# Attention scores on TensorE: one 64-row product per head in place of a block-diagonal product per pair of heads

## The chip, the core and the metric

The kernel runs on one core of a Trainium2 chip. Its engines work side by side, each with its own queue: PE (TensorE, the matrix unit; PEld is its loading of the stationary operand), DVE (VectorE), ACT (ScalarE), POOL (GpSimd) and SP (SyncE, which here only issues DMAs). The metric is the device time of one execution in microseconds (us); smaller is better.

## The reference

Attention with pooled keys and values is followed by a gated channel mix. There are 8 batches, 8 heads, 576 tokens and 64 elements per head. Keys and values are averaged over groups of 8 tokens, so that each head has 72 of each.

```python
k_p = k.reshape(B, H, Sp, pool, D).mean(axis=3)          # Sp = 72
v_p = v.reshape(B, H, Sp, pool, D).mean(axis=3)
scores = scale * np.matmul(q, k_p.transpose(0, 1, 3, 2)) # 576 x 72 per head, sum over 64
scores = scores - np.max(scores, axis=-1, keepdims=True)
attn = np.exp(scores)
attn = attn / (np.sum(attn, axis=-1, keepdims=True) + 1e-09)
x = np.matmul(attn, v_p)                                  # heads side by side: 512 wide
# channel mix, x_prev is x shifted by one token
xk = mu_k * x + (1.0 - mu_k) * x_prev
xr = mu_r * x + (1.0 - mu_r) * x_prev
k = np.maximum(xk @ w_k, 0.0)                             # 512 -> 1024
v = k * k @ w_v                                           # 1024 -> 512
out = 1.0 / (1.0 + np.exp(-(xr @ w_r))) * v
```

## The kernel before

The 8 x 576 = 4608 tokens are laid end to end and cut into 12 chunks of 384, and each chunk into three tiles of 128. 576 is four and a half tiles, so 4 of the 36 tiles hold the seam between two batches: 64 tokens of each. The other 32 are called whole tiles here.

A tile goes through `softmax(i)`: PE multiplies queries and pooled keys into two PSUM banks (`sc`), DVE takes the maximum of each head (L715) and subtracts it (L733), ACT takes the exponential (L738), DVE sums (L740, L743, L746), and DVE or POOL normalises. From the third chunk on the result is transposed on DVE in blocks of 32 (L780, L784), written to DRAM and fetched back turned; in the first two chunks PE transposes it (L826, and L881 for the last 8 keys of each head). `attended` multiplies with the pooled values on PE (L940), mixes with the shifted tokens on ACT, POOL and DVE (L946, L953, L966), and `x_parts` splits the result into a high and a low part (ACT L982, POOL L984). `hidden`, `gate` and `mixed` are the three weight products (L1011, L1063, L1094). In the first chunk they are true fp32 products (two passes of PE per product); later each is three fp32r products of one pass each, on the high and low parts.

The score product before: the pooled keys of a pair of heads stand in `kbd`, 128 rows by 144 columns, as two diagonal blocks (head 0 in rows 0 to 63 and columns 0 to 71, head 1 in rows 64 to 127 and columns 72 to 143; the rest is zeros, cleared once by a memset on L430). The queries of the pair, 128 rows by the tile's tokens, are the stationary operand. One fp32 product per pair gives both heads: four per whole tile, each two passes. On a seam tile there are four per half, with 64 columns of the array for each half; the program gives those the array shape 128 rows by 64 columns, and the halves alternate.

What sets the order: every engine runs its own queue in order. A planner (`Order`) makes the order while the program is built. Pieces of work are generators which tell what they need and what the next instruction costs; the planner takes the one that could start first by its costs, and among those the one with the earliest due time (the table `DUE`, and lead times such as `TILE_LEAD`). Loads are issued by SP in the order of `LOADS`, and each takes a free buffer first: `qs` has 3, so a fourth tile of queries cannot be issued before a score product has freed one, and all loads behind it in SP's queue stand still meanwhile. `SUM_BY` says which engine pools the keys and values of a batch (t: PE, v: DVE, g: POOL, L580), `NORM_BY` who normalises a tile (DVE or POOL), `BY_HEAD` the tiles whose exponentials ACT takes head by head (L724), and `LOW_BY` and `LAST_BITS_BY` who converts the weights.

The planner's price for a piece of PE work is built from these lines:

```python
def pe(n, whole=False, times=1):
    return "pe", times * (2 * max(0.109, n / 1200 + 0.002) if whole else max(0.109, n / 2383 + 0.0125)), False
```

For the scores of a part of a tile that is `pe(144, True, 4)`.

Of the kernel before, what the change touches and what calls it, by code (L numbers as in the profile page):

```python
# [8 lines left out]
F32 = mybir.dt.float32  # L9
# [4 lines left out]
ALU = mybir.AluOpType  # L14
# [27 lines left out]
    "k0 k1 q0 wr3 q2 q1 r0 c0 q3 wk0 wv6 k2 wk1 q5 v1 wk4 wv1 k3 wr2 v0 wr0 wk3 q4 wk5 v3 wk6 "  # L42
    "wk2 r1 wv3 wv4 wv2 wv5 wv7 wv0 v2 wk7 wr1 "
)

SUM_BY = {"k0": "t", "k1": "v", "v0": "t", "v1": "t", "r0": "t", "k2": "t", "k3": "t", "v2": "v", "v3": "g", "r1": "v", "k5": "v", "k4": "v", "v5": "v", "r2": "v", "v4": "g"}

NORM_BY = {0: "g", 1: "v", 2: "g", 3: "g", 7: "g", 5: "g", 4: "v", 8: "g", 6: "g"}
WARMING = 4
FILLS = ((("scored", 1), 7),)  # L50

LAST_BITS_BY = {"k": "aaavvvvv", "r": "vava", "v": "vaavaava"}
LOW_BY = {"k": "vvvggvgg", "r": "vvgv", "v": "vgvgvggg"}
BY_HEAD = (0, 2, 8)

BESIDE = (1,)
SQUARED_ON_ACT = 8
REST_BY = (1, 1, 1, 3)
# [29 lines left out]
    "constants": -31.16, "complements": 163.29, "fill 7": 127.28, "values 2 1": 57.34,  # L88
# [32 lines left out]
    "split_turned 8": 67.34, "split_turned 9": 136.19, "free_turned": -43.12, "fetch_turned 2": 63.7,  # L121
    "fill 2": -65.13, "split_turned 10": 147.03, "split_turned 11": 146.15, "softmax 14": 201.08,
    "keys 4 0": 355.88, "softmax 15": 188.81, "keys 4 1": 179.46, "softmax 16": 182.51,
}
SPARE = 3.109
SECOND = 24.0
FIRST = 22.0
PER_TOKEN = 0.1736
TILE_LEAD = 31.7186
ATT_LEAD = 34.7421  # L130


class Thread:
    __slots__ = ("due", "steps", "spare", "name", "at", "pe_at", "step", "last")

# [135 lines left out]
def act(n, func=None):  # L271
    return "act", 0.095 + n / 1200, False, func
# [11 lines left out]
def attention_then_channel_mix(  # L284
# [35 lines left out]

    full, low, high = {}, {}, {}

    kbd = [const.tile([P, NPAIR, 2 * KEYS], F32, name=f"kbd{i}") for i in range(2)]
    vbd_h = [const.tile([P, NPAIR, P], F32R, name=f"vbd_h{i}") for i in range(2)]
    vbd_l = [const.tile([P, NPAIR, P], F32R, name=f"vbd_l{i}") for i in range(2)]
    vbd_r = [const.tile([REM, 2, 4, D], F32R, name=f"vbd_r{i}") for i in range(2)]
# [887 lines left out]
```

## Time and profile before

| what | us |
|---|---|
| median of 3 runs (lowest, highest) | 623.45 (622.16, 623.87) |
| the profiled execution, its own time | 625.45 |
| span of the profile, first to last instruction | 623.6 |
| PE busy | 607.1 (97%) |
| DVE, ACT, POOL busy | 403.0, 363.7, 203.4 |

The profile gives one execution. Its own time lies 1.85 us above its span, and 2.0 us above the median. A busy time counts an instruction from its start to its modelled end; matmuls overlap, so the cost of one in a stream is read from the distance of the starts, not from its duration. A row of the timeline merges neighbours of one kind: start, length, engine, line, shape, count, and in brackets the idle time before it and what ended that. The shape 128*64 means 128 rows by 64 columns of the array.

### The profile page before, as it was taken

The numbers are of one execution on the slowest core, as the hardware profiler recorded it, in microseconds if no ns is written. First come the engines' busy times: TensorE is split into PE (matmuls) and PEld (weight loads), VectorE is DVE, ScalarE is ACT, GpSimd is POOL, SyncE is SP. The second block draws the span as 40 slices with busy tenths as digits, with TensorE's granted clock in tenths as the row PEclk, the third lists the DMA queues.
The fourth block names the chain that finished last, engine by engine and source line by source line (L and its number), as shares of the span: only waits on it lengthen the run. The fifth ranks groups of instructions, "written<-read, shape, count | busy, mean of one in ns | idle before, by whom it ended". The sixth has DMA issues, their size and how long they took to land.

```text
span 623.6 us, 8940 instructions
## 1 busy us (share of the span) xinstructions
PE 607.1 (97%) x3100; PEld 524.1 (84%) x3100; DVE 403.0 (65%) x826; ACT 363.7 (58%) x761; POOL 203.4 (33%) x292
## 2 busy tenths in 40 slices
PE   7789999999999999999999999999999999999997
PEld 6755457988988988988988988988988988988986
DVE  4789977975995844884884853794774753623511
ACT  4879975854575744774754753774654643633420
POOL 1130276326415215515614204713713313303100
PEclk9999999999899999999999999999999999999999
DMA  8997221562377132057147124049114013000001
GB/s 263 383 354 239 67 80 62 188 152 70 89 222 186 37 87 77 18 175 193 35 175 176 35 77 105 18 140 227 35 55 112 18 41 88 18 0 35 17 1 51
DMA packets 59453, 68.61 MB, mean 110 GB/s; under 512 B 11664, under 2 KB 43664, under 8 KB 59408
## 3 DMA queue, kind: packets, MB, share of 16 engines
q1 hardware_dynamic: 59264, 67.91, 36.6%
q8 instruction: 24, 0.39, 0.3%
q14 instruction: 21, 0.17, 0.1%
q10 hardware_dynamic: 144, 0.13, 0.1%
HBM read 49.75 MB, written 18.28 MB: 109 GB/s over the span
## 4 chain that ended last, share of the span: by engine, by line
PE 87%; DMA 5%; DVE 3%; POOL 2%; ACT 1%; issue 1%; SPq 0%; DVEq 0%; ACTq 0%; POOLq 0%
PE mm L1094 31%; PE mm L1011 29%; PE mm L1063 15%; PE bank L940 5%; PE sc L700 5%; DMA early_xrl<-in_vm 2%; DMA got_wk<-in_w_k 2%; DMA early_sl<-in_kT 1%; POOL xkl L984 1%; PE bank L448 1%; ACT t L946 1%; PE mm L591 1%; DVE xm L966 1%; POOL xrl L984 0%; ACT xkh L982 0%
## 5 line engine op out<-in xcount | busy, mean ns | idle before, releaser
L1011 PE MATMUL mm<-xkh,w_k 128*128 128x384 f32 x704 | 181.8, 339 | 1.5 <-ACT xkh L982 1.5
L1094 PE MATMUL mm<-w_v,sh 128*128 128x512 f32 x528 | 169.4, 391 | 0.0
L1011 PEld LDWEIGHTS mm<-xkh,w_k 128*128 128x128 f32 x704 | 127.1, 189 | 2.9 <-ACT xkh L982 1.7
L1011 PE MATMUL mm<-xkl,w_k 128*128 128x384 f32 x352 | 118.9, 338 | 1.7 <-POOL xkl L984 1.7
L1094 PEld LDWEIGHTS mm<-w_v,sh 128*128 128x128 f32 x528 | 99.2, 188 | 19.6
L1094 PE MATMUL mm<-w_v,sl 128*128 128x512 f32 x264 | 102.9, 390 | 0.0
L946 ACT ACTIVATE t<-bank,om_sb 128x384 f32<-128x384 f32 x96 | 49.8, 580 | 80.0 <-PE bank L940 78.7
L751 POOL TENSOR_TENSOR e<-e,sm 128x576 f32<-128x576 f32 x30 | 35.6, 1188 | 177.5 <-DVE sm L746 177.5
L1063 PE MATMUL mm<-w_r,xrh 128*128 128x512 f32 x264 | 84.2, 393 | 0.0
L1107 DVE TENSOR_TENSOR rs<-mm,rs 128x512 f32<-128x512 f32 (+1 forms) x37 | 24.9, 675 | 90.6 <-PE mm L1094 90.6
L966 DVE SCALAR_TENSOR_TENSOR xm<-bank,mu_sb,t 128x384 f32<-128x384 f32 x88 | 51.0, 611 | 36.9 <-POOL t L957 17.1
L1037 ACT CAST sh<-rk 128x384 fp32r<-128x384 f32 x88 | 44.8, 514 | 49.7 <-DVE rk L1031 49.4
L1011 PEld LDWEIGHTS mm<-xkl,w_k 128*128 128x128 f32 x352 | 66.6, 189 | 3.2 <-POOL xkl L984 3.2
L984 POOL TENSOR_TENSOR xkl<-xm,xkh 128x384 fp32r<-128x384 f32 x44 | 45.2, 1027 | 70.3 <-ACT xkh L982 70.1
L1039 DVE TENSOR_TENSOR sl<-rk,sh 128x384 fp32r<-128x384 f32 x88 | 51.8, 597 | 12.2 <-ACT sh L1037 10.5
L1063 PEld LDWEIGHTS mm<-w_r,xrh 128*128 128x128 f32 x264 | 49.6, 188 | 10.1
L1094 PEld LDWEIGHTS mm<-w_v,sl 128*128 128x128 f32 x264 | 49.6, 188 | 9.2
L1031 DVE SCALAR_TENSOR_TENSOR rk<-mm,rk 128x384 f32<-128x384 f32 x88 | 47.3, 548 | 11.1 <-ACT rk L1024 10.7
L1063 PE MATMUL mm<-w_r,xrl 128*128 128x512 f32 x132 | 51.4, 389 | 0.0
L1024 ACT ACTIVATE rk<-mm 128x384 f32<-128x384 f32 x88 | 42.2, 487 | 10.8 <-PE mm L1011 7.4
L984 POOL TENSOR_TENSOR xrl<-xm,xrh 128x384 fp32r<-128x384 f32 x44 | 45.6, 1036 | 3.3 <-ACT xrh L982 3.3
L580 POOL TENSOR_TENSOR stage<-stage 128x512 f32<-128x512 f32 (+5 forms) x51 | 45.0, 897 | 1.2
(126 smaller groups left out, 904.2 us busy)
## 6 DMA issues: line engine op xcount, KB each, us to landing
out<-rs SPq DMA_DIRECT2D x35, 256.0 KB, 2.0
passing<-pm SPq DMA_DIRECT2D x30, 288.0 KB, 2.2
qs<-in_qT SPq DMA_DIRECT2D x32, 256.0 KB, 3.6
stage<-in_kT SPq DMA_DIRECT2D x14, 576.0 KB, 4.7
turned_sb<-passing SPq DMA_DIRECT2D x40, 192.0 KB, 4.3
stage<-in_vm SPq DMA_DIRECT2D x14, 512.0 KB, 6.5
got_wk<-in_w_k SPq DMA_DIRECT2D x8, 512.0 KB, 9.0
got_wv<-in_w_v SPq DMA_DIRECT2D x8, 512.0 KB, 11.2
```

The lines of the kernel that those rows point to most:

```text
L580: nc_eng.tensor_tensor(out=st[:, :, :w], in0=st[:, :, :w], in1=st[:, :, w:2 * w], op=ALU.add)
L751: eng.tensor_tensor(out=e, in0=e, in1=sm.broadcast_to([P, 2, 4, KEYS]), op=ALU.mult)
L946: nc.scalar.activation(out=t[:, m, 1:n + 1], in_=xp, func=AF.Copy, scale=om_sb[:, m, g:g + 1])
L966: nc.vector.scalar_tensor_tensor(out=xm[:, :n], in0=xp, scalar=mu_sb[:, m, g:g + 1], in1=t[:, m, :n], op0=ALU.mult, op1=ALU.add,)
L984: nc.gpsimd.tensor_tensor(out=lo, in0=xm[:, :n], in1=hi, op=ALU.subtract)
L1011: nc.tensor.matmul(out=hp, lhsT=w[:, o], rhs=x[:, ct, o_t], start=(ct == 0 and k == 0), stop=(ct == NCT - 1 and k == len(terms) - 1),)
L1024: nc.scalar.activation(out=rk[:, :n], in_=hp, func=AF.Relu)
L1031: nc.vector.scalar_tensor_tensor(out=rk[:, :n], in0=hp, scalar=0.0, in1=rk[:, :n], op0=ALU.max, op1=ALU.mult)
L1037: nc.scalar.copy(out=sh, in_=rk[:, :n])
L1039: nc.vector.tensor_tensor(out=operand("sl", c)[:, jt, o_t], in0=rk[:, :n], in1=sh, op=ALU.subtract)
L1063: nc.tensor.matmul(out=bank, lhsT=x[:, ct, o], rhs=w, start=(ct == 0 and k == 0), stop=(ct == NCT - 1 and k == len(terms) - 1),)
L1094: nc.tensor.matmul(out=bank, lhsT=s[:, o], rhs=w, start=(jt == 0 and k == 0), stop=(jt == NJT - 1 and k == len(terms) - 1),)
```

## The change

The pooled keys become dense: `ks` holds, for each pair, head 0 in rows 0 to 63 and head 1 in rows 64 to 127, both in the same 72 columns. The score of each head is a product of its own over 64 rows: 8 products of 72 columns per part of a tile instead of 4 of 144. The two heads of a pair use the upper and the lower half of the array's rows and write to different banks (`halves[h2]`); the program gives these products the array shape 64 by 128 on whole tiles and 64 by 64 on seam tiles. The order on a seam tile is now part by part, and head by head inside a part. The layout of scores, exponentials and normalised tiles follows: even heads, then odd heads. One copy writes the keys of two pairs (before: two copies of 64 rows), and the memsets of `kbd` go. The planner is told 0.75 us per part (`SCORE`), and its tables differ.

```diff
 LOADS = (
-    "k0 k1 q0 wr3 q2 q1 r0 c0 q3 wk0 wv6 k2 wk1 q5 v1 wk4 wv1 k3 wr2 v0 wr0 wk3 q4 wk5 v3 wk6 "
-    "wk2 r1 wv3 wv4 wv2 wv5 wv7 wv0 v2 wk7 wr1 "
+    "k0 k1 q0 wr3 q1 q3 r0 c0 wk0 wv6 q2 v1 wk1 k2 wk4 k3 q5 wv1 v0 wr2 wk3 wk2 wr0 v3 q4 wk5 "
+    "wk6 v2 wv4 r1 wk7 wv5 wv2 wr1 wv7 wv0 wv3 "
 )
-SUM_BY = {..., "v2": "v", "v3": "g", ..., "r2": "v", "v4": "g"}
+SUM_BY = {..., "v2": "g", "v3": "g", ..., "r2": "v", "v4": "v"}
-NORM_BY = {0: "g", 1: "v", 2: "g", 3: "g", 7: "g", 5: "g", 4: "v", 8: "g", 6: "g"}
+NORM_BY = {0: "v", 1: "v", 2: "v", 3: "v", 7: "g", 5: "g", 4: "v", 8: "v", 6: "g"}
-FILLS = ((("scored", 1), 7),)
+FILLS = ((("scored", 1), 8),)
-LAST_BITS_BY = {"k": "aaavvvvv", "r": "vava", "v": "vaavaava"}
-LOW_BY = {"k": "vvvggvgg", "r": "vvgv", "v": "vgvgvggg"}
-BY_HEAD = (0, 2, 8)
+LAST_BITS_BY = {"k": "avavvavv", "r": "aava", "v": "vaavavvv"}
+LOW_BY = {"k": "vvvvvvvg", "r": "gvgg", "v": "vgvvgvgv"}
+BY_HEAD = (0, 2, 6, 8)
-SQUARED_ON_ACT = 8
+SQUARED_ON_ACT = 5
 DUE = {
-    "keys 0 0": -9.94, "values 0 0": 24.5, "keys 0 1": -129.19, "values 0 1": -72.82,
+    "keys 0 0": 81.0, "values 0 0": -2.56, "keys 0 1": -144.43, "values 0 1": -63.22,
...
-SPARE = 3.109
+SPARE = 2.8473
+SCORE = 0.75
-PER_TOKEN = 0.1736
-TILE_LEAD = 31.7186
-ATT_LEAD = 34.7421
+PER_TOKEN = 0.1794
+TILE_LEAD = 54.3891
+ATT_LEAD = 35.0556
...
-    kbd = [const.tile([P, NPAIR, 2 * KEYS], F32, name=f"kbd{i}") for i in range(2)]
+    ks = [const.tile([P, NPAIR, KEYS], F32, name=f"ks{i}") for i in range(2)]
...
-        for b in range(2):
-            yield "pool" if b else "dve", 0.6, False
-            (nc.gpsimd if b else nc.vector).memset(kbd[b], 0.0)
-            order.make(("kbd clear", b))
...
-        yield "act", 0.53, False
-        for h2 in range(2):
-            r = slice(h2 * D, (h2 + 1) * D)
-            nc.scalar.copy(out=kbd[b % 2][r, gs, h2 * KEYS:(h2 + 1) * KEYS], in_=o[r])
+        yield act(2 * KEYS)
+        nc.scalar.copy(out=ks[b % 2][:, gs], in_=o)
...
-        yield pe(2 * KEYS, True, NPAIR * len(parts))
-        for g in range(NPAIR):
-            k = (g % 2) * 2 * KEYS
-            for b, _, n, o in parts:
-                nc.tensor.matmul(
-                    out=halves[g // 2][o:o + n, 0, k:k + 2 * KEYS],
-                    lhsT=qs[:, g, o:o + n], rhs=kbd[b % 2][:, g, :], start=True, stop=True,
-                )
+        yield "pe", SCORE * len(parts), False
+        for b, _, n, o in parts:
+            for g in range(NPAIR):
+                for h2 in range(2):
+                    r = slice(h2 * D, (h2 + 1) * D)
+                    nc.tensor.matmul(
+                        out=halves[h2][o:o + n, 0, g * KEYS:(g + 1) * KEYS],
+                        lhsT=qs[r, g, o:o + n], rhs=ks[b % 2][r, g, :], start=True, stop=True,
+                    )
...
-        pairs = e.rearrange("p a (h two) k -> p (a h) two k", two=2)
         for h2 in range(2):
             nc.vector.transpose(
...
-                in_=pairs[:, :, h2, :KM].rearrange("p g (f j) -> p f g j", j=BLOCK),
+                in_=e[:, h2, :, :KM].rearrange("p g (f j) -> p f g j", j=BLOCK),
             )
```

The changed tables move instructions. Chunks are counted from 0. From chunk 4 on, the blocks of PE's queue stand as before, with 8 products in place of 4 per part of a tile; in chunks 2 and 3 two blocks of scores stand at another place between the weight products. Two other places differ where engines wait. The first is SP's queue at the start, right behind the small load of `mu_sb` (`qs` are queries, `got_wk` and `got_wv` weights, `in_kT` keys, `in_vm` values; the number tells the buffer). Before:

```order
L491 DMA mu_sb<-in_mu 128x8
L499 DMA qs_105<-in_qT 128x4x128
L509 DMA got_wk_174<-in_w_k 128x1024
L509 DMA got_wv_186<-in_w_v 128x1024
L523 DMA early_sl<-in_kT 128x1152
L509 DMA got_wk_191<-in_w_k 128x1024
```

With the change:

```order
L489 DMA mu_sb<-in_mu 128x8
L507 DMA got_wk_153<-in_w_k 128x1024
L507 DMA got_wv_156<-in_w_v 128x1024
L497 DMA qs_105<-in_qT 128x4x128
L521 DMA early_sl<-in_vm 128x1024
L507 DMA got_wk_186<-in_w_k 128x1024
```

The queries that reuse the first tile's buffer `qs_105` now stand behind two weights, where they stood ahead of them.

The second is POOL's queue while the inputs of chunk 2's weight products are made (`xkl` and `xrl` are low parts, `stage` the values of batch 2 on their way to being pooled, `t` the shifted tokens). Before:

```order
L984 TENSOR_TENSOR xrl_1208<-xm_82,xrh_1207 128x384
L580 TENSOR_TENSOR stage_108<-stage_108 128x2x256
L580 TENSOR_TENSOR stage_108<-stage_108 128x2x128
L580 TENSOR_TENSOR stage_108<-stage_108 128x2x64
L580 TENSOR_TENSOR stage_110<-stage_110 96x2x256
L953 COPY t_80<-carry 128x2
L580 TENSOR_TENSOR stage_110<-stage_110 96x2x128
L984 TENSOR_TENSOR xkl_1199<-xm_83,xkh_1198 128x384
```

With the change:

```order
L981 TENSOR_TENSOR xrl_1253<-xm_83,xrh_1252 128x384
L578 TENSOR_TENSOR stage_110<-stage_110 128x2x256
L578 TENSOR_TENSOR stage_110<-stage_110 128x2x128
L578 TENSOR_TENSOR stage_110<-stage_110 128x2x64
L578 TENSOR_TENSOR stage_108<-stage_108 96x2x256
L578 TENSOR_TENSOR stage_108<-stage_108 96x2x128
L578 TENSOR_TENSOR stage_108<-stage_108 96x2x64
L578 TENSOR_TENSOR stage_109<-stage_109 128x2x256
L950 COPY t_81<-carry 128x2
L981 TENSOR_TENSOR xkl_1244<-xm_82,xkh_1243 128x384
```

Seven sums stand between the last `xrl` of the third pair and the copy for the fourth, where four stood.

More of the change, by code (lines that the diff above doesn't have):

```diff
@@ L41 @@
 LOADS = (
-    "k0 k1 q0 wr3 q2 q1 r0 c0 q3 wk0 wv6 k2 wk1 q5 v1 wk4 wv1 k3 wr2 v0 wr0 wk3 q4 wk5 v3 wk6 "
-    "wk2 r1 wv3 wv4 wv2 wv5 wv7 wv0 v2 wk7 wr1 "
-)
-SUM_BY = {"k0": "t", "k1": "v", "v0": "t", "v1": "t", "r0": "t", "k2": "t", "k3": "t", "v2": "v", "v3": "g", "r1": "v", "k5": "v", "k4": "v", "v5": "v", "r2": "v", "v4": "g"}
-NORM_BY = {0: "g", 1: "v", 2: "g", 3: "g", 7: "g", 5: "g", 4: "v", 8: "g", 6: "g"}
+    "k0 k1 q0 wr3 q1 q3 r0 c0 wk0 wv6 q2 v1 wk1 k2 wk4 k3 q5 wv1 v0 wr2 wk3 wk2 wr0 v3 q4 wk5 "
+    "wk6 v2 wv4 r1 wk7 wv5 wv2 wr1 wv7 wv0 wv3 "
+)
+SUM_BY = {"k0": "t", "k1": "v", "v0": "t", "v1": "t", "r0": "t", "k2": "t", "k3": "t", "v2": "g", "v3": "g", "r1": "v", "k5": "v", "k4": "v", "v5": "v", "r2": "v", "v4": "v"}
+NORM_BY = {0: "v", 1: "v", 2: "v", 3: "v", 7: "g", 5: "g", 4: "v", 8: "v", 6: "g"}
 WARMING = 4
-FILLS = ((("scored", 1), 7),)
-LAST_BITS_BY = {"k": "aaavvvvv", "r": "vava", "v": "vaavaava"}
-LOW_BY = {"k": "vvvggvgg", "r": "vvgv", "v": "vgvgvggg"}
-BY_HEAD = (0, 2, 8)
+FILLS = ((("scored", 1), 8),)
+LAST_BITS_BY = {"k": "avavvavv", "r": "aava", "v": "vaavavvv"}
+LOW_BY = {"k": "vvvvvvvg", "r": "gvgg", "v": "vgvvgvgv"}
+BY_HEAD = (0, 2, 6, 8)
 BESIDE = (1,)
-SQUARED_ON_ACT = 8
-REST_BY = (1, 1, 1, 3)
+SQUARED_ON_ACT = 5
+REST_BY = (1, 1, 3)
 TURNED = 2
@@ L62 @@
 DUE = {
[25 rows of a table removed]
-    "constants": -31.16, "complements": 163.29, "fill 7": 127.28, "values 2 1": 57.34,
[32 rows of a table removed]
-    "split_turned 8": 67.34, "split_turned 9": 136.19, "free_turned": -43.12, "fetch_turned 2": 63.7,
-    "fill 2": -65.13, "split_turned 10": 147.03, "split_turned 11": 146.15, "softmax 14": 201.08,
-    "keys 4 0": 355.88, "softmax 15": 188.81, "keys 4 1": 179.46, "softmax 16": 182.51,
-}
-SPARE = 3.109
[58 rows of a table added]
+    "split_turned 7": 99.44, "split_turned 8": 73.38, "split_turned 9": 148.16, "free_turned": -68.37,
+    "fetch_turned 2": 53.56, "fill 2": -42.7, "split_turned 10": 156.94, "split_turned 11": 160.34,
+    "softmax 14": 181.95, "keys 4 0": 382.77, "softmax 15": 207.62, "keys 4 1": 196.24,
+    "softmax 16": 179.15,
+}
+SPARE = 2.8473
+SCORE = 0.75
 SECOND = 24.0
 FIRST = 22.0
-PER_TOKEN = 0.1736
-TILE_LEAD = 31.7186
-ATT_LEAD = 34.7421
+PER_TOKEN = 0.1794
+TILE_LEAD = 54.3891
+ATT_LEAD = 35.0556
 class Thread:
@@ L609, in keys @@
     def keys(b, p):
-        yield need(("k", 2 * b + p), *([("scored", last_tile[b - 2])] if b > 1 else [("kbd clear", b)]))
+        yield need(("k", 2 * b + p), *([("scored", last_tile[b - 2])] if b > 1 else []))
         kind, raw, o = yield from sums(held.pop(("k", 2 * b + p)), KEYS, SUM_BY.get(f"k{2 * b + p}", "v"))
         gs = slice(2 * p, 2 * p + 2)
-        yield "act", 0.53, False
-        for h2 in range(2):
-            r = slice(h2 * D, (h2 + 1) * D)
-            nc.scalar.copy(out=kbd[b % 2][r, gs, h2 * KEYS:(h2 + 1) * KEYS], in_=o[r])
+        yield act(2 * KEYS)
+        nc.scalar.copy(out=ks[b % 2][:, gs], in_=o)
         done_with(kind, raw)
@@ L756, in softmax @@
         got = yield take("pm")
-        pm = got[:, :8 * KM].rearrange("p (a h k) -> p a h k", a=2, h=4)
+        pm = got[:, :8 * KM].rearrange("p (g two k) -> p g two k", g=NPAIR, two=2)
         yield dve(8 * KR) if v else ("pool", 0.24, True)
         eng.tensor_tensor(
-            out=px, in0=e[:, :, :, KM:], in1=sm.broadcast_to([P, 2, 4, KR]), op=ALU.mult
+            out=px.rearrange("p a (g two) k -> p two (a g) k", two=2), in0=e[:, :, :, KM:], in1=sm.broadcast_to([P, 2, 4, KR]), op=ALU.mult
         )
@@ L765, in softmax @@
         eng.tensor_tensor(
-            out=pm, in0=e[:, :, :, :KM], in1=sm.broadcast_to([P, 2, 4, KM]), op=ALU.mult
+            out=pm.rearrange("p g two k -> p two g k"), in0=e[:, :, :, :KM], in1=sm.broadcast_to([P, 2, 4, KM]), op=ALU.mult
         )
@@ L781, in turned @@
                 out=u[:, h2 * 8 * BLOCK:(h2 + 1) * 8 * BLOCK].rearrange("p (f g j) -> p f g j", f=2, j=BLOCK),
-                in_=pairs[:, :, h2, :KM].rearrange("p g (f j) -> p f g j", j=BLOCK),
+                in_=e[:, h2, :, :KM].rearrange("p g (f j) -> p f g j", j=BLOCK),
             )
         nc.vector.transpose(
-            out=u[:, 16 * BLOCK:].rearrange("p (r h k) -> p r h k", r=2, k=KR), in_=e[:, :, :, KM:]
+            out=u[:, 16 * BLOCK:].rearrange("p (g two k) -> p g two k", two=2, k=KR),
+            in_=e[:, :, :, KM:].rearrange("p two g k -> p g two k"),
         )
@@ L827, in transposed @@
                 out=tp[:, g, :],
-                in_=pm[:, g // 2, (g % 2) * 2:(g % 2) * 2 + 2, :].rearrange("p h k -> p (h k)"),
+                in_=pm[:, g].rearrange("p h k -> p (h k)"),
                 identity=ident,
```

113 rows, old and new, of the table DUE are left out of this document.

## The prediction

> **What bounds the kernel now.** I read the page first: busy times, the span in slices and the chain that ended last.
>
> ```profile
> PE 607.1 (97%) x3100; PEld 524.1 (84%) x3100; DVE 403.0 (65%) x826; ACT 363.7 (58%) x761; POOL 203.4 (33%) x292
> PE   7789999999999999999999999999999999999997
> PE 87%; DMA 5%; DVE 3%; POOL 2%; ACT 1%; issue 1%; SPq 0%; DVEq 0%; ACTq 0%; POOLq 0%
> ```
>
> PE is the bound, and not only on average: after the first four slices (62 us) hardly a slice falls under 9, and the chain runs over PE for 87% of the span. What PE's stream gains or loses after the start moves the end one to one. The windows and the timeline show two exceptions.
>
> ```profile
> 20.00:40.00 20.00, 17.54 (x123) 14.28 (x122) 16.48 (x37) 16.06 (x49) 6.34 (x13) 1.00 1.04 366
> 40.00:56.00 16.00, 14.89 (x51) 8.31 (x50) 14.56 (x33) 15.19 (x30) 0.65 (x2) 1.00 0.99 353
> 56.00:70.00 14.00, 13.21 (x42) 6.93 (x41) 13.61 (x31) 13.52 (x27) 1.75 (x2) 1.00 0.26 85
> 157.00:160.00 3.00, 3.00 (x11) 3.00 (x12) 2.58 (x5) 1.97 (x6) 2.82 (x4) 0.57 0.01 2
> ...
> 153.27 1.14 PE L700 MATMUL sc<-kbd,qs 128*128 128x144 f32 x8
> 155.89 0.62 PE L1011 MATMUL mm<-xkh,w_k 128*128 128x384 f32 x2 [1.48 <-ACT xkh L982]
> 156.97 0.44 PE L1011 MATMUL mm<-xkl,w_k 128*128 128x384 f32 x1 [0.46 <-POOL xkl L984]
> ```
>
> The columns of the windows are PE, PEld, DVE, ACT, POOL, the granted clock, the DMA share and GB/s. Up to 70 us DVE and ACT are full (13.6 and 13.5 of 14 us), and the DMAs up to 56 us. Around 156 us PE waits 1.48 + 0.46 = 1.94 us for the last input of chunk 2's first weight product, and then runs at a granted clock of 0.57 for 3 us.
>
> **The score block before.** A whole tile, from the timeline, with two rows of the chain that give the step of the other products in a stream:
>
> ```profile
> 266.17 0.33 PE L1011 MATMUL mm<-xkl,w_k 128*128 128x384 f32 x1
> 266.34 1.14 PE L700 MATMUL sc<-kbd,qs 128*128 128x144 f32 x8
> ...
> 267.78 0.63 PE L1063 MATMUL mm<-w_r,xrh 128*128 128x512 f32 x2
> ...
> 202.07 16.66 PE mm L1011 x96
> ...
> 267.48 8.20 PE mm L1063 x36
> ```
>
> A pass of 384 columns steps by 16.66 / 96 = 0.174 us, one of 512 by 8.20 / 36 = 0.228 us. From 266.17 to the third pass behind the block at 267.78 are 1.61 us. Less one step of 0.174 and two of 0.228 that leaves 0.98 us: 8 passes of 0.1225, or 144 columns in 0.12 us, so 1.2 columns per ns. Nothing is lost at either edge. A seam tile uses another array shape:
>
> ```profile
> 295.46 0.33 PE L940 MATMUL bank<-ptr,vbd_r 96*128 96x384 f32 x1
> 295.72 1.20 PE L700 MATMUL sc<-kbd,qs 128*64 128x144 f32 x16
> 296.85 0.62 PE L1011 MATMUL mm<-xkh,w_k 128*128 128x384 f32 x2
> 297.31 0.33 PE L1011 MATMUL mm<-xkl,w_k 128*128 128x384 f32 x1
> ...
> 295.72 0.93 PEld L700 LDWEIGHTS sc<-kbd,qs 128*64 128x64 f32 x16 [0.25 <-issue]
> 296.85 0.30 PEld L1011 LDWEIGHTS mm<-xkh,w_k 128*128 128x128 f32 x2 [0.20 <-issue]
> ```
>
> From 295.46 to 297.31 are 1.85 us; less three steps of 0.174 the block takes 1.33. Its 16 passes fit into 8 rounds of 0.1225 = 0.98 (twice 8 passes in 1.20 us), so the two halves do run beside each other. The other 0.35 us lies at the edges, and the loads show it: both the first load of the block and the first behind it start late, with nothing to wait for but "issue". I read this as the price of going into another array shape and back: loads that otherwise run ahead of the products don't start before the array has finished.
>
> **The score block after.** 16 passes of 72 columns per whole tile, two heads side by side, so 8 rounds. The products alone would take 72 / 1.2 = 0.06 us, with the step's 0.0025 us 0.0625. The loads:
>
> ```profile
> L700 PEld LDWEIGHTS sc<-kbd,qs 128*128 128x128 f32 x248 | 33.7, 189 | 4.0 <-ACT e L724 1.3 <-ACT kbd L616 0.9 <-issue 0.5
> L940 PEld LDWEIGHTS bank<-ptr,vbd_r 96*128 96x128 f32 x64 | 12.1, 190 | 0.5
> L700 PEld LDWEIGHTS sc<-kbd,qs 128*64 128x64 f32 x64 | 3.7, 136 | 1.1 <-issue 0.7 <-DVE got_wk L548 0.4
> ```
>
> 64 columns fewer take 189 - 136 = 53 ns off, and 32 rows fewer nothing. So a load of 128 columns holds its port about 0.107 us whatever its rows, and 64 rows of queries by 128 tokens are no cheaper than 128 rows. Each pass has its own load. I take 0.109 us per round, the load and not the product: 7 x 0.109 + 0.0625 = 0.826. To it comes the shape's price, 0.352, and 0.055 because the first load, which is not hidden, is 128 columns long instead of 64. That is 1.23 us against 0.98: **+0.25 us per whole tile**. The change halves what PE multiplies and not what it loads. (In the Trainium skill, TensorE: Matmul & The Clock Gate, LDWEIGHTS, says that a load's time goes by its columns and not by the contraction rows; TensorEngine Tiling (Array Packing), Key Properties, says that "Changing tiling mode (not just tile) drains the TensorE". The three rows and the two "issue" gaps agree; both rules speak against this change, and by them the block is the 1.23.)
>
> Bounds per whole tile. Below: no price for the shape, and loads that don't bind, 8 x 0.0625 = 0.50, so -0.48. Above: the loads of the two halves one after the other, 16 x 0.109 + 0.407 = 2.15, so +1.17. I stay near the seam row, which shows another shape and loads side by side on this very line.
>
> Which tiles count: 20 whole tiles after the stall at 156 us, and 5 between 70 and 140 us. Two more, at 147.59 and 153.27 us, run into the stall, which hides 0.5 us. The 5 before 70 us lie in the start. 25 x 0.25 = **+6.3 us**. Seam tiles: 16 passes per part now go two at a time over the rows, part after part, so 16 rounds of 0.0625 = 1.0 and the same 0.35: 1.35 against 1.33, nothing.
>
> **The stall at 156 us.** POOL and DVE in the timeline, and the sums of L580 there (ns: shortest, median, longest):
>
> ```profile
> 149.73 3.90 POOL L580 TENSOR_TENSOR stage<-stage 128x512 f32<-128x512 f32 x4
> 153.57 0.25 POOL L953 COPY t<-carry 128x2 f32<-128x2 f32 x1
> 155.92 1.00 POOL L984 TENSOR_TENSOR xkl<-xm,xkh 128x384 fp32r<-128x384 f32 x1 [1.42 <-ACT xkh L982]
> ...
> 154.68 0.62 DVE L966 SCALAR_TENSOR_TENSOR xm<-bank,mu_sb,t 128x384 f32<-128x384 f32 x1
> ...
> L580 POOL TENSOR_TENSOR stage<-stage x5: 462/732/1302, 149.7 to 153.8; 128x512 f32<-128x512 f32 x1, 128x256 f32<-128x256 f32 x1, 128x128 f32<-128x128 f32 x1, 96x512 f32<-96x512 f32 x1
> ```
>
> Four sums stand ahead of the copy that DVE's L966 needs; with the change seven. The three more are a middle, a short and a long one: 0.73 + 0.46 + 1.30 = 2.5 us. The copy then ends at 153.82 + 2.5 = 156.3, and L966, which starts at 154.68 now, starts 1.6 us later. Behind it wait ACT's L982, POOL's L984 and PE. **+1.6 us**; it could be 0 if POOL gets to these sums earlier, and 2.5 at most.
>
> **The start.** SP's queue:
>
> ```profile
> 5.84 0.70 SPq L491 DMA_DIRECT2D mu_sb<-in_mu  x1
> 10.19 0.55 SPq L499 DMA_DIRECT2D qs<-in_qT  x1
> 10.78 0.62 SPq L509 DMA_DIRECT2D got_wk<-in_w_k  x1
> ```
>
> SP stands from 6.5 to 10.2 us, since the next queries need the buffer of the first tile, and every load stands behind them. With the change two weights of 512 KB are issued before that wait. Up to 56 us the start is short of DMA, so the hole is worth something: 1.05 MB at the 353 GB/s of the row above are 3.0 us at most. Against it, DVE takes the normalisation of tiles 0, 2 and 3 and three squarings more, in a stretch where it has 97% to do:
>
> ```profile
> L765 DVE TENSOR_TENSOR pm<-e,sm 128x512 f32<-128x512 f32 x2 | 1.4, 686 | 0.0
> L1031 DVE SCALAR_TENSOR_TENSOR rk<-mm,rk 128x384 f32<-128x384 f32 x88 | 47.3, 548 | 11.1 <-ACT rk L1024 10.7
> L580 DVE TENSOR_TENSOR stage<-stage 128x512 f32<-128x512 f32 x2 | 2.4, 1176 | 0.0
> ```
>
> That is 3 x 0.69 + 3 x 0.55 = 3.7 us; it gives up the sums of one load of values (`v2`), 1.2 us for the long one of three and some 2 for all. I take -3.0 + 1.7, about **-1 us**, with -4.4 and +3.7 as bounds: by the windows PE idles 2.5 + 1.1 + 0.8 = 4.4 us between 20 and 70 us, and more than that is hardly won there. The rest costs nothing that counts: one more filling product falls into the start's idle time, and the single copy of the keys on ACT, at 58%, is shorter than two.
>
> **Sum.** 6.3 + 1.6 - 1 = +6.9 us on the profiled execution of 625.45, which makes 632.3. That execution is 2.0 us above the median of the runs, so the forecast in their terms is **630 us**.
>
> **The rivals.**
>
> *The shape costs nothing, and the block gets cheaper.* This ends on the other side. For it: the transposes of the last keys also have 64 columns, and stand in a stream without a gap.
>
> ```profile
> 21.27 0.61 PE L458 MATMUL bank<-ident 128*128 128x128 f32 x4
> 21.72 0.27 PE L881 MATMUL bank<-ident,px 128*64 128x128 f32 x1
> 21.82 0.39 PE L458 MATMUL bank<-ident 128*128 128x128 f32 x2
> ```
>
> 0.11 us from start to start on both sides, the step of the 128-column products next to them. If rows are like this, the block is 8 x 0.109 = 0.87 us, and 25 x -0.11 - 1 + 1.6 makes 621; if the loads don't bind either it is 0.50, and the time 612. The planner's own price of 0.75 lies between (25 x -0.23 + 0.6 = -5.2, so 618); its old price, 4 x 2 x 0.122 = 0.98, is just what the trace shows. It decides as soon as the block falls under 0.95. Against it: the transposes don't use two places of the array at once, while the seam block does, as the change would, and there both gaps are seen. (By the Trainium skill, TensorEngine Tiling (Array Packing), Theoretical Speedup, a dimension of up to 64 gives up to 2 times; the best case above is that rule, and no row here shows it for rows of the array.)
>
> *The halves don't overlap.* If the two heads' loads or products go one after the other, the change doesn't do what it says: 2.15 us per block, 25 x 1.17 = 29 us, 653. Against it: the seam's halves, in the same queue, alternate without loss.
>
> *The block costs as forecast, but the start wins all that PE idles there.* 6.3 - 4.4 and no longer stall: about 2 us slower, 625, at the edge of what can be told from no change.
>
> **How the numbers follow.** Forecast 0.50, with a range of its own from 626 to 635. Cheap block 0.29. No overlap 0.10. Start wins all 0.11, most of it within 0.3% (1.9 us, about what a measurement of this kernel can tell from no change). So faster 0.29, same 0.10, slower 0.61. The range from 613 to 637 leaves out the case without overlap, the cheapest blocks and a forecast gone wrong twice.
>
> **What would show it.** Right: PE's rows of the score block show 16 starts in 8 pairs about 0.11 us apart, the first load behind "issue" gaps of 0.2 to 0.25 us on both sides, and some 1.23 us from the pass before to the pass behind. Wrong: pairs 0.06 us apart, no gap on PEld, or single starts. The stall would show in PE's wait for `xkl` near 156 us, 3 to 4 us long, and the start in the time of chunk 0's first gate product (70.19 us now). If the block is right and the time is not, the start or the stall was mis-sized.

## The result, and the profile after

| | before | after |
|---|---|---|
| median, us (lowest, highest) | 623.66 (622.16, 624.2) | 630.21 (629.36, 630.76) |
| after / before (95% interval) | | 1.0108 (1.0086 to 1.0129) |
| span of the profiled execution | 623.6 | 627.6 |

The change makes the kernel slower by 1.1%, 6.5 us. The forecast was 630. The two profiled executions differ by 4.0 us only: that of the change is the fastest of its four, that of before lies 2.0 us above its median. The page of the kernel after, with the busy times, PE's slices and the engines' shares of the chain that ended last:

```profile
PE 612.8 (98%) x3422; PEld 521.4 (83%) x3422; DVE 408.7 (65%) x838; ACT 359.7 (57%) x758; POOL 194.9 (31%) x281
PE   8899999998999999999999999999999999999997
PE 84%; DMA 4%; DVE 4%; POOL 3%; ACT 3%; issue 1%; SPq 1%; DVEq 0%; POOLq 0%; ACTq 0%
```

PE was the bound and still is. The zeros of the score product are gone, and PE is 5.7 us busier, with 322 passes more (320 of them are scores).

**The block of a whole tile**, from the timelines of PE and PEld:

```profile
211.00 0.34 PE L1008 MATMUL mm<-xkl,w_k 128*128 128x384 f32 x1
211.27 1.11 PE L697 MATMUL sc<-ks,qs 64*128 64x72 f32 x16
212.31 0.62 PE L1008 MATMUL mm<-xkh,w_k 128*128 128x384 f32 x2
212.77 0.33 PE L1008 MATMUL mm<-xkl,w_k 128*128 128x384 f32 x1
...
210.83 0.19 PEld L1008 LDWEIGHTS mm<-xkl,w_k 128*128 128x128 f32 x1
211.26 0.97 PEld L697 LDWEIGHTS sc<-ks,qs 64*128 64x128 f32 x16 [0.25 <-issue]
212.31 0.30 PEld L1008 LDWEIGHTS mm<-xkh,w_k 128*128 128x128 f32 x2
```

From 211.00 to the third pass behind the block at 212.77 are 1.77 us. Less three steps of 0.174 that leaves 1.25 us for the block, against 0.98 before: +0.27. The single records of this block start at 0, 0.007, 0.167, 0.173, 0.278, 0.285, and so on up to 0.837 and 0.843 us: 16 passes in 8 pairs, the second pair 0.167 us behind the first, the others 0.105 to 0.112 us apart. The last pair at 0.837 and its 0.0625 us make 0.90, so 0.35 us lie at the two edges. Ahead of the block PEld shows the forecast gap of 0.25 us. Behind it, the first load starts 0.08 us after the last one has ended (212.31 against 212.23), not the forecast 0.2. Both halves load and multiply side by side, and each round lasts about as long as the prediction's estimate for a load of 128 columns (0.107 us). The load of 64 rows is no cheaper than the one of 128 rows (187 here, 189 ns before):

```profile
L697 PEld LDWEIGHTS sc<-ks,qs 64*128 64x128 f32 x496 | 30.1, 187 | 9.7 <-issue 6.5 <-DVE stage L578 0.7 <-ACT ks L612 0.6
L697 PEld LDWEIGHTS sc<-ks,qs 64*64 64x64 f32 x128 | 3.5, 132 | 1.1 <-issue 1.1
```

**A seam tile**, from PE's timeline:

```profile
296.94 0.33 PE L937 MATMUL bank<-ptr,vbd_r 96*128 96x384 f32 x1
297.21 1.03 PE L697 MATMUL sc<-ks,qs 64*64 64x72 f32 x32
298.17 0.62 PE L1008 MATMUL mm<-xkh,w_k 128*128 128x384 f32 x2
298.62 0.34 PE L1008 MATMUL mm<-xkl,w_k 128*128 128x384 f32 x1
```

From 296.94 to 298.62, less three steps: 1.16 us, where 1.33 stood before and 1.35 was forecast. The rounds of the first part are 0.0625 us apart as forecast (behind a first one of 0.113). But the second part's passes, on the other 64 columns of the array, begin 0.31 us behind the start of the block, while the first part's rounds go on until 0.49.

**The stall near 156 us**, with POOL, DVE and PE of the kernel after:

```profile
146.82 6.45 POOL L578 TENSOR_TENSOR stage<-stage 128x512 f32<-128x512 f32 x7
153.22 0.25 POOL L950 COPY t<-carry 128x2 f32<-128x2 f32 x1
...
149.92 1.75 DVE L632 TENSOR_TENSOR vbd_l<-stage,vbd_h 64x128 fp32r<-64x128 f32 x2
...
153.50 0.62 DVE L963 SCALAR_TENSOR_TENSOR xm<-bank,mu_sb,t 128x384 f32<-128x384 f32 x1
...
145.79 1.11 PE L697 MATMUL sc<-ks,qs 64*128 64x72 f32 x16
...
154.71 0.62 PE L1008 MATMUL mm<-xkh,w_k 128*128 128x384 f32 x2 [1.86 <-ACT xkh L979]
155.79 0.44 PE L1008 MATMUL mm<-xkl,w_k 128*128 128x384 f32 x1 [0.46 <-POOL xkl L981]
```

and two rows of the kernel before that the prediction does not show:

```profile
147.59 1.14 PE L700 MATMUL sc<-kbd,qs 128*128 128x144 f32 x8
...
152.75 1.90 DVE L636 TENSOR_TENSOR vbd_l<-stage,vbd_h 64x128 fp32r<-64x128 f32 x2 [2.43 <-ACT vbd_h L631]
```

POOL's seven sums take 6.45 us where four took 3.90, as forecast. Counted from the score block ahead, though (145.79 after, 147.59 before), POOL begins them at 1.03 us instead of 2.14. Before, the copy ended at 153.82 and DVE's L966 started 0.86 us later, since DVE was busy with L636 until 154.65; after, its L632 is done at 151.67, the copy ends at 153.47 and L963 starts at 153.50. So the path to PE grows by 2.55 - 1.11 - 0.83 = 0.6 us. PE's waits are 1.86 + 0.46 = 2.32 us against 1.94. From the start of that score block to the `xkl` product behind the stall are 10.00 us, before 9.38: +0.6, two longer score blocks included. Behind the stall the granted clock is low in both: 0.57 from 157 to 161 us before, 0.51 from 156.5 to 160 us after, which is 1.7 us of full clock each time.

From the `xkl` product behind the stall to the end of the span: 627.6 - 155.8 = 471.8 us, before 623.6 - 157.0 = 466.7. That is +5.1, and 20 whole tiles by 0.27 less three seam tiles by 0.17 make 4.9.

### The profile page after: what moved, and what is told of

It is laid out like the page before. It is cut to its first block, busy times and chain, and to the rows that moved or that the text cites. A ratio compares the mean times of both kernels' runs of the same rounds, so it can differ in the third digit from the quotient of the medians.

```text
span 627.6 us, 9557 instructions
## 1 busy us (share of the span) xinstructions
PE 612.8 (98%) x3422; PEld 521.4 (83%) x3422; DVE 408.7 (65%) x838; ACT 359.7 (57%) x758; POOL 194.9 (31%) x281
## 4 chain that ended last, share of the span: by engine, by line
PE 84%; DMA 4%; DVE 4%; POOL 3%; ACT 3%; issue 1%; SPq 1%; DVEq 0%; POOLq 0%; ACTq 0%
PE mm L1091 30%; PE mm L1008 29%; PE mm L1060 15%; PE bank L937 5%; PE sc L697 5%; DMA early_ptl<-in_kT 2%; DMA stage<-in_vr 1%; POOL xkl L981 1%; POOL stage L578 1%; DMA stage<-in_kT 1%; ACT t L943 1%; DVE xm L963 1%; ACT xkh L979 1%; DVE stage L578 1%; POOL xrl L981 0%
## 5 line engine op out<-in xcount | busy, mean ns | idle before, releaser
L963 DVE SCALAR_TENSOR_TENSOR xm<-bank,mu_sb,t 128x384 f32<-128x384 f32 x88 | 51.1, 612 | 36.4 <-POOL t L954 15.0
L1036 DVE TENSOR_TENSOR sl<-rk,sh 128x384 fp32r<-128x384 f32 x88 | 57.0, 653 | 10.0 <-ACT sh L1034 8.3
```

Source lines behind the costliest of these rows:

```text
L963: nc.vector.scalar_tensor_tensor(out=xm[:, :n], in0=xp, scalar=mu_sb[:, m, g:g + 1], in1=t[:, m, :n], op0=ALU.mult, op1=ALU.add,)
L1036: nc.vector.tensor_tensor(out=operand("sl", c)[:, jt, o_t], in0=rk[:, :n], in1=sh, op=ALU.subtract)
```

## The experiments

Each ratio is to runs of the kernel before, beside it on the same chip. Their median was 624.27 us beside `product_alone`, `old_product_new_tables`, `late_values` and `after_again`, 623.70 beside the two `extra` kernels and `wide_120`, and 623.21 beside `old_product_sp_tail` and the two `quarters`.

### The product without the tables, and the tables without the product

`product_alone`: the dense keys and the products of the change, with all tables and prices of the kernel before. PE's blocks then stand in the order of before.

```diff
-        yield "pe", SCORE * len(parts), False
+        yield pe(2 * KEYS, True, NPAIR * len(parts))
```

(shown against the changed kernel, together with the tables of before)

> The new score product in the order of before: tables, loads and the planner's prices are those of before, so that every engine's order stays as it was; the memsets of the old keys are gone. Theory (the block itself is dearer): 25 whole tiles on PE's path at 1.25 us instead of 0.98, which are +6.8, seams about 0.17 us cheaper each, -0.5 for three: 6.3 us slower than before, about 630, and the start as before. Rival (the tables cost the time, by a worse order): within 2 us of before, 622 to 626.

Measured: 631.11 us (630.41 to 632.21), ratio 1.0110 (1.0094 to 1.0125). The product alone costs 6.8 us, all that the change costs, and near the 6.3 expected. Its blocks are spaced like those of the change, record by record; the stall nearly vanishes:

```profile
156.75 0.62 PE L1009 MATMUL mm<-xkh,w_k 128*128 128x384 f32 x2 [0.21 <-ACT xkh L980]
157.83 0.44 PE L1009 MATMUL mm<-xkl,w_k 128*128 128x384 f32 x1 [0.46 <-POOL xkl L982]
```

The longer blocks ahead of it use up most of it (0.60 us of waiting for DVE come behind the next seam tile instead), and still the kernel is no faster than with the tables of the change. What the tables give or take in sum is thus smaller than the block by far.

`old_product_new_tables`: the block-diagonal product of before, in the order, tables and prices of the change.

> The block-diagonal product of before in the order of the change: its tables and the planner's prices for scores and keys. Theory: the 6.3 us of the blocks are given back and what the start gained stays (2.9 us by the first product of the last kind in chunk 0, 72.67 us against 75.58): 621 to 624, so at or under before. Rival (the order is what costs): 629 to 631, as the change.

Measured: 626.82 us (625.6 to 627.89), ratio 1.0039 (1.0024 to 1.0055): 2.5 us slower than before, so the 621 to 624 expected was missed, and so was the rival's 629 to 631. The end of its timeline (PE, DVE and the issues of SP and ACT), and the last row of the kernel before:

```profile
618.60 0.39 PE L1095 MATMUL mm<-w_v,sh 128*128 128x512 f32 x1
619.10 0.76 DVE L1108 TENSOR_TENSOR rs<-mm,rs 128x256 f32<-128x256 f32 x2 [4.75 <-PE mm L1095]
619.55 0.33 SPq L1110 DMA_DIRECT2D out<-rs  x1
620.22 2.39 ACTq L1110 DMA_DIRECT2D out<-rs  x1
```

```profile
620.71 0.37 ACTq L1109 DMA_DIRECT2D out<-rs  x1
```

PE is done 0.8 us earlier than in the profile of before, but ACT's issue of the last half tile takes 2.39 us instead of 0.37. From PE's last product to the end of the span are 6.5 us, in the kernel before 4.3.

`old_product_sp_tail`: the same kernel, with that half tile sent by SP.

```diff
-            yield ("act", 0.1, False) if h else ("sp", 0.6, False)
-            (nc.scalar if h else nc.sync).dma_start(out=out[at:at + P, o], in_=rs[:, o])
+            yield "sp", 0.6, False
+            nc.sync.dma_start(out=out[at:at + P, o], in_=rs[:, o])
```

> old_product_new_tables with one edit: the second half of the last output tile is sent by SP's queue instead of ACT's, whose issue took 2.39 us there and 0.37 in every other kernel. If that issue made the kernel 2 us longer: 624.5 to 625.5, within 0.3% of the kernel before, and the time from PE's last product to the end 4.3 to 5 us against 6.5. Rival, something that all late transfers meet there: it stays at 626 to 627, with a tail of 6 us or more.

Measured: 624.57 us (623.49 to 626.15), ratio 1.0015 (1.0004 to 1.0026).

```profile
618.36 0.39 PE L1095 MATMUL mm<-w_v,sh 128*128 128x512 f32 x1
618.86 0.75 DVE L1108 TENSOR_TENSOR rs<-mm,rs 128x256 f32<-128x256 f32 x2 [4.75 <-PE mm L1095]
619.31 0.81 SPq L1110 DMA_DIRECT2D out<-rs  x2
```

The span ends at 622.7, 4.3 us behind the last product, as elsewhere. So the slow issue made most of the excess: 0.24% between the two ratios, 1.5 us (a rough size, since their intervals just overlap). What is left, +0.9 us (0.2 to 1.6), is the tables' own cost with the old product. The stall is 2.58 + 0.46 = 3.04 us with ACT's issue and with SP's, 1.1 us more than in the kernel before. Why ACT's issue is slow in that one program stays open; the profile names nothing that it waits for.

`late_values`: `old_product_new_tables`, with the values of batch 3 held back until chunk 2's first weight product is placed, so that POOL's sums no longer stand ahead of the copy.

```diff
+        if b == 3:
+            yield need(("hid", 2, 0, 0))
```

(in `values` and in `last_values`)

> The same, and the pooling of batch 3's values may not begin before chunk 2's first weight product is done; they are needed two chunks later. Theory: POOL's seven sums, 6.4 us, no longer stand between the third and the fourth pair's inputs, so PE's wait of 1.9 us and the slow clock behind it (1.5 us) go: 2 to 3.5 us less than the kernel with the old product and the new tables. Rival: the fourth pair is late anyway, or the sums delay something else later: no change.

Measured: 625.5 us (623.74 to 626.93), ratio 1.0022 (1.0010 to 1.0033), 1.3 us under its base, where 2 to 3.5 were expected: missed. This kernel also has a normal tail (4.4 us), so most of the gain is not the stall's: PE ends only 0.6 us earlier. PE's timeline shows where the stall went:

```profile
158.92 1.20 PE L705 MATMUL sc<-kbd,qs 128*64 128x144 f32 x16 [1.64 <-DVE e L738]
...
162.26 0.62 PE L1016 MATMUL mm<-xkh,w_k 128*128 128x384 f32 x2 [2.13 <-DVE rk L1036]
```

Three score blocks now stand close together and wait for the banks `sc` to be read, and later PE waits for DVE. 3.04 us went and 3.77 came: in this stretch PE is ahead of its helpers, and moving one piece moves the wait.

### The price of the array shape, and of a round

`extra_128` and `extra_64`: the kernel before, with one product of 8 columns (overwritten at once by the scores) ahead of each whole tile's scores; over 128 rows in one, over 64 rows in the other. Only the other array shape tells them apart. The edit of the second:

```diff
+        if len(parts) == 1:
+            nc.tensor.matmul(
+                out=halves[0][:, 0, :8], lhsT=qs[:64, 0, :], rhs=kbd[parts[0][0] % 2][:64, 0, :8],
+                start=True, stop=True,
+            )
```

> The kernel before, with one small product more ahead of the scores of each whole tile: 8 columns, all 128 rows, overwritten by the scores behind it. It measures two loads of 128 columns in the common array shape: 2 x 0.109 us on 25 to 27 tiles of PE's path, 5.5 to 5.9 us: about 629.

> The same small product over the upper 64 rows only, so in the array shape 64 by 128 and back. Theory (the shape has a price at both edges, 0.41 us with the unhidden first load): 0.41 + 0.11 + 0.01 = 0.53 us per tile, 25 to 27 tiles: 13 to 14 us, about 637, 8 us above the kernel with 128 rows. Rival (the shape costs nothing): as with 128 rows, 629.

Measured: 629.07 us, ratio 1.0086 (1.0069 to 1.0102), and 636.08 us, ratio 1.0205 (1.0181 to 1.0230): 5.4 and 12.4 us. PE's timeline around one tile, of `extra_128` and then of `extra_64`:

```profile
217.63 0.33 PE L1016 MATMUL mm<-xkl,w_k 128*128 128x384 f32 x1
217.80 0.28 PE L698 MATMUL sc<-kbd,qs 128*128 128x8 f32 x2
...
219.47 0.62 PE L1068 MATMUL mm<-w_r,xrh 128*128 128x512 f32 x2
```

```profile
220.31 0.34 PE L1016 MATMUL mm<-xkl,w_k 128*128 128x384 f32 x1
220.58 0.39 PE L698 MATMUL sc<-kbd,qs 64*128 64x8 f32 x2
...
222.45 0.62 PE L1068 MATMUL mm<-w_r,xrh 128*128 128x512 f32 x2
```

From the pass ahead to the row behind are 1.84 and 2.14 us: the one product over 64 rows between products over 128 rows costs 0.30 us (0.29 by the unrounded records in 18 of the 20 whole tiles behind 165 us, 0.26 in two). 7.0 us over 25 whole tiles agree with that. Against the kernel before, 2.14 less one step of 0.174 and two of 0.228 is 1.51 us, 0.53 more than 0.98, as expected. The price is paid for the visit to the other shape: nothing else in these two kernels differs. The rival by which the shape is free has fallen.

`wide_120`: the changed kernel with products of 120 columns instead of 72 (the 48 more are overwritten by the next pair; behind the last pair stand zeros).

```diff
-                        out=halves[h2][o:o + n, 0, g * KEYS:(g + 1) * KEYS],
+                        out=halves[h2][o:o + n, 0, g * KEYS:g * KEYS + WIDE],
...
-                        lhsT=qs[r, g, o:o + n], rhs=ks[b % 2][r, g, :], start=True, stop=True,
+                        lhsT=qs[r, g, o:o + n],
+                        rhs=ks[b % 2].rearrange("p g k -> p (g k)")[r, g * KEYS:g * KEYS + WIDE],
```

> The change, with products of 120 columns in place of 72: the 48 more are the next keys, and each is overwritten by the next head's product, so the scores stay what they are. Theory (the load sets the round of 0.112 us, and the product's 0.0625 hides in it): a product of 120 columns takes 0.1025 us, still under the load; only the last one of a block shows, 0.04 us per tile: 630 to 632. Rival (the rounds are set by the products and something per product): 8 x 0.04 = 0.32 us per tile, 25 tiles, 8 us: 638.

Measured: 630.2 us, ratio 1.0103 (1.0088 to 1.0118), the time of the change. With two thirds more columns the rounds of a whole tile are still 0.105 to 0.112 us apart; only the first grows, from 0.167 to 0.207, and the block from 1.25 to 1.29 us. So a round is not the product's time; the load sets it. On seam tiles, whose loads have 64 columns, the wider products do cost time: 1.64 us for 1.16. By these rows the kernel should be some 2.4 us slower than the change; the median does not show them, and why is open (its profile reaches the first product of `mixed` at 71.3 us, that of the change at 72.5).

`after_again`: the changed kernel once more beside these.

> The change itself, beside the others on the same chip: 6 to 7 us slower than before, about 630.

Measured: 630.93 us (628.94 to 632.75), ratio 1.0106 (1.0088 to 1.0124). Its profile and the first one of the same kernel part in the start, and the granted clock shows where (first the windows of `after`, then of `after_again`, with the columns of the prediction's windows):

```profile
25.00:28.60 3.60, 3.60 (x39) 3.37 (x38) 3.02 (x7) 2.27 (x9) 0.00 (x0) 1.00 1.03 411
25.00:28.60 3.60, 3.60 (x17) 3.37 (x16) 2.75 (x8) 1.28 (x6) 0.00 (x0) 0.53 1.03 407
```

The second is 0.5 us behind the first ahead of this stretch and 2.2 us behind it afterwards, through the same products; at the first product of `mixed` it is 2.5 us.

### Four quarters instead of two halves

The seam tiles were cheaper than forecast because four quarters of the array worked at once for a moment. `quarters` does so on purpose: every score block is written as 64 by 64, a whole tile's tokens as two halves of 64, and the four products of a pair of heads stand one behind the other. `quarters_old_order` does the same with the tables of the kernel before (the base is `product_alone`).

```diff
-        for b, _, n, o in parts:
-            for g in range(NPAIR):
+        quarters = parts if len(parts) == 2 else [(parts[0][0], 0, 64, o) for o in (0, 64)]
+        for g in range(NPAIR):
+            for b, _, n, o in quarters:
```

> The changed kernel, with every score block written for four quarters of the array (64 rows by 64 columns): a whole tile's 128 tokens as two halves of 64, and the four products of a pair (two heads, two halves of tokens) one behind the other, 32 products per tile; seam tiles in the same order. Theory 'a round is set by the loads of one half of the rows, which share their way': the loads of 64 columns take 0.055 us each, two per half of the rows and pair, so a pair of heads' time is again 0.11 us, the block 1.22 to 1.25 us and the time that of the change, 630 to 631. Rival 'a load belongs to its quarter': 8 rounds of 0.0625 to 0.07 + 0.35 for the shape, 0.85 to 0.95 us per whole tile, 0.3 to 0.4 less than the change on each of 25: 620 to 623.

> The same four quarters, in the order and with the tables of the kernel before (product_alone's base, 631.1 with two halves). Loads shared: 630 to 631.5. A load belongs to its quarter: the whole-tile block is 0.85 to 0.95 us against 0.98 in the kernel before, so 25 x (-0.03 to -0.13) - 3 x 0.3 or so for the seams: 1.5 to 4 us under the kernel before.

Measured: `quarters` 621.29 us (620.3 to 622.63), ratio 0.9963 (0.9948 to 0.9978); `quarters_old_order` **620.48 us** (619.02 to 621.68), ratio 0.9950 (0.9933 to 0.9966). Both beat both kernels of this case, the second the kernel before by 0.5%. These are the times expected for loads that belong to their quarter. A whole tile of it, on PE and PEld, and a seam tile:

```profile
215.41 0.34 PE L1010 MATMUL mm<-xkl,w_k 128*128 128x384 f32 x1
215.68 0.73 PE L699 MATMUL sc<-ks,qs 64*64 64x72 f32 x32
216.34 0.50 PE L1062 MATMUL mm<-w_r,xrh 128*128 128x512 f32 x1
216.67 0.40 PE L1062 MATMUL mm<-w_r,xrl 128*128 128x512 f32 x1
216.91 0.39 PE L1062 MATMUL mm<-w_r,xrh 128*128 128x512 f32 x1
...
215.67 0.58 PEld L699 LDWEIGHTS sc<-ks,qs 64*64 64x64 f32 x32 [0.25 <-issue]
```

```profile
291.93 0.33 PE L939 MATMUL bank<-ptr,vbd_r 96*128 96x384 f32 x1
292.19 0.73 PE L699 MATMUL sc<-ks,qs 64*64 64x72 f32 x32
292.85 0.62 PE L1010 MATMUL mm<-xkh,w_k 128*128 128x384 f32 x2
293.31 0.34 PE L1010 MATMUL mm<-xkl,w_k 128*128 128x384 f32 x1
```

From 215.41 to 216.91 are 1.50 us, less 0.174 and two of 0.228: 0.87 us; the seam tile is 1.38 less three of 0.174, 0.86. The records come in fours, 0.007 us apart inside and 0.0625 us from one four to the next (0.113 behind the first): now the product sets the round, and the loads of all four quarters go side by side. The gap at the edge is still there. Against before that is 25 by -0.11 and 3 by -0.47, together -4.2 us; 3.1 (2.1 to 4.2) were measured. Against the change, `quarters` should win 25 by 0.38 and 3 by 0.29, 10.4 us; 1.45% were won, 9.0 us. The row of `quarters` at the stall, from PE's timeline:

```profile
154.13 1.01 PE L1009 MATMUL mm<-xkh,w_k 128*128 128x384 f32 x2 [4.13 <-ACT xkh L980]
```

PE waits 4.13 us where the change had 2.32, since it arrives earlier at inputs that are no sooner ready: the 1.8 us given back there are more than the difference.

## Why the prediction was right

- **The block** was the cause, in the size forecast: 1.25 us (1.23 forecast), +0.27 per whole tile. `product_alone` shows that nothing else is needed for the 6.5 us. Its parts hold too: the round is the load's (`wide_120`), the load of 64 rows is as long as that of 128 (187 ns), and the halves go side by side. The forecast gap of 0.2 us behind the block does not show on PEld (0.08), but the two edges together cost the 0.35 us read off the seam block.
- **The price of the shape** was read as 0.35 us off the two edges of a seam block; `extra_64` less `extra_128` measures 0.29 for one product alone, over the 0.23 that it costs in the common shape. The block's sum, 1.23, is 0.02 us short of the measured 1.25: its rounds are 0.90 us long, with the 0.167 of the first, where 0.826 + 0.055 = 0.88 was taken. The rule that was weighed against the change, a drain for every change of the tiling mode (the Trainium skill, TensorEngine Tiling (Array Packing), Key Properties), is borne out by these two runs. It does not show everywhere: the transposes of 64 columns, which the prediction shows between products of the full shape, have no gap.
- **The seam tiles** were mis-sized: "16 rounds of 0.0625 = 1.0 and the same 0.35: 1.35 against 1.33, nothing" measured 1.16, a gain of 0.17. The step took the two parts as one after the other. They overlap, as their starts show. On three tiles it is 0.5 us.
- **The stall**, forecast at +1.6, gave about +0.6. The three sums more did cost 2.5 us on POOL. But POOL started them 1.1 us earlier against the score block, which the step named as its way to fail ("it could be 0 if POOL gets to these sums earlier"). PE's wait there is 2.3 us, where 3 to 4 were named as the sign. And with the old product the same tables have a stall of 3.04 us: the longer score blocks ahead of it hide 0.7 of that.
- **The start**, forecast at -1 within -4.4 and +3.7, is not settled. Two of its readings were loose. DVE is full only from 56 to 70 us; the windows have 82% of it busy from 20 to 40 and 91% from 40 to 56. And the first product of chunk 0's gate is at 62.57 us in the profile before; 70.19 is where the chain enters the last ten of them. In the first profile of the change chunk 0's first product of `mixed` comes 2.9 us earlier than in the profile of before (72.5 and 75.4 us), in a second profile of the same kernel 0.4 earlier (75.0), so single profiles can't size it. Most of what parts these two profiles is the granted clock (see `after_again`). Over all profiles, the seven with the tables of the change reach this product at 71.3 to 75.0 us (median 72.5), the five with the tables of before at 73.3 to 76.1 (median 75.2). That speaks for a gain. The sums leave it none: 25 by 0.27, less 3 by 0.17, and 0.6 are 6.8 of the 6.5 measured.
- So 630 came out as near as it did because errors of 0.5 (block), -0.5 (seams), -1.0 (stall) and +1 (start, if it is worth nothing) us cancel. That is luck; the sign and the bulk rest on the block alone.
- The rivals: the cheap block falls by 8 pairs at 0.11 us with 0.35 us at the edges; the halves that don't overlap fall by the pairs 0.007 us apart; a start that wins everything falls by `product_alone`, which has the start of before and the same time. The cheap block was not far off in another shape: `quarters` has it at 0.87 us.

## What to carry to other kernels

Here, splitting a product over the array's rows halved what is multiplied and left the time of a load as it was: with a load per product, as many columns in the load as before and short products, the round stays as long as the load, and each visit to the other shape cost some 0.3 us on top. Count loads by their columns, and if a shape must be entered anyway, split columns as well as rows, with the quarters in turn, so that the loads get shorter with the products. Where PE waits for helpers, a faster block ahead of the wait only makes the wait longer (4.13 us in `quarters`): take the gain from the tiles behind it.

## What had not been expected

- Four quarters load and multiply at once: 64-column loads of 132 to 135 ns in fours, 0.0625 us from four to four, against 0.11 us for pairs of 128-column loads. (The Trainium skill, TensorEngine Tiling (Array Packing), Key Properties, says that different tiles can load and multiply in parallel; the runs agree. A half of the rows still takes 0.11 us for 128 columns.)
- One issue of a DMA on ACT, of the same size and place as in the kernel before, took 2.39 us instead of 0.37. Only one profile shows it; that the kernel's median fell by 0.24% with SP in its place speaks for it in the other executions.
- Two executions of the changed kernel differ by 2.5 us at the first product of `mixed`, more than the 0.9 us that the tables changed in the medians; 1.7 us of it come in one stretch at a granted clock of 0.53.
- The slow clock does not follow from the wait alone. Behind the same stall of 3.04 us it is 0.53 from 155.0 to 158.6 us in `old_product_new_tables` and 1.00 in `old_product_sp_tail`. What sets it off in one execution and not in the other is open.
